# Layer norm without its division: mean only in the norm, the weight folded into the next weights, the division on the last pass's sums, and GpSimd alone for block preparation and residual adds

## The chip, the cores and the metric

One core of one Trainium2 chip. The metric is the device time of one launch in microseconds, the median of several runs. TensorE is called PE here, VectorE DVE, ScalarE ACT, GpSimd POOL or GpSimd, and SP is the engine whose queue issues the DMAs.

## The reference, cut to what matters

```
x = attention(q, k, v), keys and values pooled by 8      (8 batches, 576 tokens, 512 columns)
u = x + (x^T U V)^T                                       (mixing along the tokens, rank 32)
x = u + max(u w1, 0) w2                                   (layer 0: 512 -> 2048 -> 512)
mu = mean(x); var = mean((x - mu)^2)                      (along the 512 columns)
xn = (x - mu) / sqrt(var + 1e-6) * g
out = x + max(xn w1', 0) w2'                              (layer 1: 512 -> 2048 -> 512)
```

All in float32. The scale of a token is positive, so max(s a, 0) = s max(a, 0): the division by the root can stand before or behind layer 1.

## The kernel before, in words

The 4608 tokens stand on the free axis, the 512 columns as 4 chunks (NCC) of 128 partitions. A float32 product is made of three matmuls on rounded parts, high times high, low times high and high times low; `split` makes the high part by a rounding copy (on ACT or DVE) and the low part by a subtraction (on DVE or GpSimd).

Phase A (up to about 650 us) computes attention, the token mixing and the first 8 of the 16 hidden blocks of layer 0. `ahead` decodes later weights from float64 words and stores them in DRAM (`w_d`).

Then come three passes, each over 9 groups of 512 tokens (TG): pass 0 is the other half of layer 0, passes 1 and 2 are the halves of layer 1. A group has 4 units, a unit being two hidden blocks. `unit` makes the first product of a unit by a scheme with 7 block products instead of 8 (42 matmuls of 256 columns into the PSUM tiles `pa` and `pbc`, with the joins on DVE at lines 1315 and 1321, the activations on ACT at 1279 and their low parts on DVE at 1285). `second` issues the 24 matmuls of the second product (512 columns, PSUM tiles `py`) one unit later, between those of the next `unit`. So a unit is 66 matmuls. The join of line 1321 reads and writes the PSUM tile into which the last block product then adds: PE waits there for DVE.

- `group_prep` loads a group (`xraw`), makes the differences of blocks (line 1212, tiles `t3`, `t2` and `xraw`) and the 7 pairs of parts `op`. There are 16 `op` buffers and a group takes 14, so most of the next group's parts are made while the last unit of the present one runs.
- `residual` loads `res` and `yt` and adds them (line 1397). `finish` adds the four PSUM sums (line 1360) and stores. Pass 0 stores to `x_d`, pass 1 keeps its partial sum in `p_d`, pass 2 adds everything and writes the output.
- `norm` treats a group of pass 0 during the next group, in two halves of 256 tokens: sum of the chunks, split, mean by two matmuls with a matrix of 1/512 (lines 1418 and 1419), subtraction (1442), squares on ACT and their sum (1453, 1454), the same two matmuls again, then a root on ACT (1461), a reciprocal on DVE (1466), one correcting step (1468 to 1474) and a multiplication by the weight g and the reciprocal (1481). The result goes to `n_d`, from which passes 1 and 2 read.

The order of all instructions is made by the class `Order` while the program is built: each operation has a cost for every engine that may take it, a due time that follows the PE work recorded so far, and the buffers that it holds; the planner simulates queues and buffers and issues whatever is ready with the earliest due time, on the engine that would end it first. The engines then run these lists in order; what waits at the head of a list holds up all behind it.

Of the kernel before, what the change touches and what calls it, by code (L numbers as in the profile page):

```python
# [386 lines left out]

class Kern:
    def __init__(self, nc, tc, aps):
# [62 lines left out]
        for a in ("lnh", "lnl"):  # L452
            ring(b2, a, [128, TH], F32R)
        for a in ("lns", "lnq", "lnm", "lnv", "lnd"):
            ring(b2, a, [128, TH])
# [8 lines left out]
    def setup(self, ctx):  # L464
# [9 lines left out]
        self.eps = cp.tile([128, 1], F32, tag="eps", name="eps")  # L474
        nc.gpsimd.memset(self.eps, 1e-6)
        self.neg_b = cp.tile([128, 1], F32, tag="negb", name="neg_b")
# [9 lines left out]
        self.p_d = [dp.tile([128, NCC, TG], F32, tag=f"p_d{g}", name=f"p_d{g}") for g in range(NG)]  # L486
        self.w_d = {}
# [195 lines left out]
    def ahead(self, layer, f, z):  # L683

        x = self.decoded(layer, f, z)
        self.wd[layer, f, z] = d = Buf(None)
# [516 lines left out]
    def group_prep(self, p, g):  # L1203
# [24 lines left out]
        def sp(k):  # L1228
# [6 lines left out]
            self.split(View(hl[0], None, view), View(hl[1], None, view), src, TG)  # L1235
# [129 lines left out]
    def residual(self, p, g):  # L1365
# [27 lines left out]
        )  # L1393
        for c in range(NCC):
            o.op(
                {GP: c_pool(TG), DVE: c_dve(TG)},
# [5 lines left out]
    def norm(self, g):  # L1402

        nc, o = self.nc, self.o
        x = self.res[g]
        steps = []
        eng = {GP: c_pool(TH), DVE: c_dve(TH)}
        for z in range(2):
            t = slice(z * TH, z * TH + TH)
            b = {}  # L1410

            def total(b=b):
                hi, lo, ps = self.buf("lnh"), self.buf("lnl"), self.buf("pbc")
                whole = lambda t: t
                self.split(View(hi, None, whole), View(lo, None, whole), View(b["s"], None, whole), TH)

                def mm(e):
                    e.matmul(ps.t[:, :TH], self.ones, hi.t, start=True, stop=False)
                    e.matmul(ps.t[:, :TH], self.ones, lo.t, start=False, stop=True)

                o.op({PE: c_pe(TH, 2)}, mm, r=[hi, lo], w=[ps])
                return ps

            def n0(b=b, t=t):
                s, q = b["s"], b["q"] = self.buf("lns"), self.buf("lnq")
                o.op(eng, lambda e: e.tensor_add(s.t, x.t[:, 0, t], x.t[:, 1, t]), r=[(x, 0), (x, 1)], w=[s])
                o.op(eng, lambda e: e.tensor_add(q.t, x.t[:, 2, t], x.t[:, 3, t]), r=[(x, 2), (x, 3)], w=[q])
                o.op(eng, lambda e: e.tensor_add(s.t, s.t, q.t), r=[q], w=[s])

            def n2(b=b, t=t, total=total):  # L1430
                ps = total()
                mu = self.buf("lnm")
                o.op(
                    {ACT: c_act(TH, True), DVE: c_dve(TH)},
                    lambda e: copy(nc, e, mu.t, ps.t[:, :TH]),
                    r=[ps],
                    w=[mu],
                )
                for c in range(NCC):
                    o.op(  # L1440
                        eng,
                        lambda e, c=c: e.tensor_sub(x.t[:, c, t], x.t[:, c, t], mu.t),
                        r=[mu],
                        w=[(x, c)],
                    )

            def n4(b=b, t=t):
                s = b["s"] = self.buf("lns")
                sq = {ACT: c_act(TH)}
                o.op(sq, lambda e: e.activation(s.t, x.t[:, 0, t], AF.Square), r=[(x, 0)], w=[s])  # L1450
                for c in range(1, NCC):
                    q = self.buf("lnq")
                    o.op(sq, lambda e, c=c, q=q: e.activation(q.t, x.t[:, c, t], AF.Square), r=[(x, c)], w=[q])
                    o.op(eng, lambda e, q=q: e.tensor_add(s.t, s.t, q.t), r=[q], w=[s])

            def n6(b=b, total=total):
                ps = total()
                sd, ve = b["sd"], b["ve"] = self.buf("lnd"), self.buf("lnv")
                o.op(
                    {ACT: c_act(TH, True) + 40},  # L1460
                    lambda e: e.activation(sd.t, ps.t[:, :TH], AF.Sqrt, bias=self.eps),
                    r=[ps],
# [144 lines left out]
```

## Time and profile before

| | |
|---|---|
| median of 3 runs | 1839.62 us (1839.45 to 1840.44) |
| profiled execution, its own time | 1839.23 us |
| its span, first to last instruction | 1837.4 us |
| PE busy / weight loads | 1769.2 us (96%) / 1619.5 us (88%) |
| DVE busy | 1279.1 us (70%), 2512 instructions |
| ACT busy | 723.4 us (39%), 2047 instructions |
| GpSimd busy | 435.6 us (24%), 446 instructions |
| pass 0, 1 and 2 begin (first matmul of line 1257 in each) | 652.4, 1063.8 and 1448.6 us |

Busy is the time in which an engine executes; a PE that is busy at the lower of its two clocks counts as busy. Share of busy time alone does not say where the time goes: the stages differ, and the table of windows and the list of waits tell them apart.

### The profile page before, as it was taken

The numbers are of one execution on the slowest core, as the hardware profiler recorded it, in microseconds if no ns is written. First come the engines' busy times: TensorE is split into PE (matmuls) and PEld (weight loads), VectorE is DVE, ScalarE is ACT, GpSimd is POOL, SyncE is SP. The second block draws the span as 40 slices with busy tenths as digits, with TensorE's granted clock in tenths as the row PEclk, the third lists the DMA queues.
The fourth block names the chain that finished last, engine by engine and source line by source line (L and its number), as shares of the span: only waits on it lengthen the run. The fifth ranks groups of instructions, "written<-read, shape, count | busy, mean of one in ns | idle before, by whom it ended". The sixth has DMA issues, their size and how long they took to land.

```text
span 1837.4 us, 30175 instructions
## 1 busy us (share of the span) xinstructions
PE 1769.2 (96%) x11482; PEld 1619.5 (88%) x11482; DVE 1279.1 (70%) x2512; ACT 723.4 (39%) x2047; POOL 435.6 (24%) x446
## 2 busy tenths in 40 slices
PE   5689999999999999999999999999999999999999
PEld 4579999999999998888888888999999999999998
DVE  7987888888855577888888898776434754454443
ACT  4445655655644233333333453333332432222221
POOL 2242322323310122222222331111111321111110
PEclk7689999999999999999999999999999999999999
DMA  6434444444411352333333334434111433222211
GB/s 179 152 114 154 137 153 155 138 154 149 124 62 46 111 192 81 115 115 115 115 115 115 115 127 138 132 127 142 53 64 58 160 116 115 93 92 92 98 64 47
DMA packets 88642, 212.42 MB, mean 116 GB/s; under 512 B 9264, under 2 KB 17456, under 8 KB 82736
## 3 DMA queue, kind: packets, MB, share of 16 engines
q1 hardware_dynamic: 88352, 210.49, 34.8%
q8 instruction: 90, 1.47, 0.3%
q14 instruction: 56, 0.46, 0.1%
q10 hardware_dynamic: 144, 0.00, 0.0%
HBM read 141.25 MB, written 69.21 MB: 115 GB/s over the span
## 4 chain that ended last, share of the span: by engine, by line
PE 87%; DVE 9%; DMA 1%; ACT 1%; issue 1%; POOL 0%; SPq 0%; DVEq 0%; ACTq 0%; POOLq 0%
PE py L1345 30%; PE pa L1257 15%; PE pbc L1257 12%; PE pa L1027 11%; PE pbc L1060 10%; PE py L378 3%; PE py L767 2%; PE py L871 1%; DVE lnv L1468 1%; DVE res L1481 1%; DVE lnd L1466 1%; PE py L889 1%; PE py L890 1%; PE py L928 0%; DMA v<-v 0%
## 5 line engine op out<-in xcount | busy, mean ns | idle before, releaser
L1345 PE MATMUL py<-hid,w2h 128*128 128x512 f32 x1728 | 546.4, 398 | 0.0
L1257 PE MATMUL pa<-op,w1h 128*128 128x256 f32 x1728 | 328.5, 282 | 21.5 <-DVE pa L1321 19.8
L1257 PEld LDWEIGHTS pa<-op,w1h 128*128 128x128 f32 x1728 | 294.0, 189 | 59.4 <-DVE pa L1321 22.6
L1345 PE MATMUL py<-hid,w2l 128*128 128x512 f32 x864 | 337.9, 391 | 0.0
L1345 PEld LDWEIGHTS py<-hid,w2h 128*128 128x128 f32 x1728 | 278.7, 191 | 13.4
L1257 PE MATMUL pbc<-op,w1h 128*128 128x256 f32 x1296 | 247.2, 283 | 1.3 <-ACT s L383 0.6
L1257 PEld LDWEIGHTS pbc<-op,w1h 128*128 128x128 f32 x1296 | 221.9, 190 | 28.5 <-DVE lnv L1465 0.8
L1257 PE MATMUL pa<-op,w1l 128*128 128x256 f32 x864 | 244.2, 283 | 0.0
L1027 PE MATMUL pa<-hid,wh 128*128 128x288 f32 x1024 | 220.1, 307 | 8.9 <-DVE op L1039 8.8
L1060 PE MATMUL pbc<-op,wh 128*128 128x288 f32 x1024 | 215.8, 303 | 0.0
L1315 DVE TENSOR_TENSOR pbc<-s,pbc 128x512 f32<-128x512 f32 x108 | 74.8, 692 | 183.2 <-PE pbc L1257 183.1
L1345 PEld LDWEIGHTS py<-hid,w2l 128*128 128x128 f32 x864 | 163.4, 189 | 36.6
L1257 PE MATMUL pbc<-op,w1l 128*128 128x256 f32 x648 | 183.7, 283 | 0.0
L1027 PEld LDWEIGHTS pa<-hid,wh 128*128 128x128 f32 x1024 | 167.1, 192 | 12.3 <-DVE op L1039 8.7
L1279 ACT ACTIVATE hid<-pbc 128x512 fp32r<-128x512 f32 x108 | 64.7, 599 | 266.4 <-DVE pbc L1315 265.6
L1060 PEld LDWEIGHTS pbc<-op,wh 128*128 128x128 f32 x1024 | 163.7, 188 | 4.4 <-issue 2.8
L1257 PEld LDWEIGHTS pa<-op,w1l 128*128 128x128 f32 x864 | 163.4, 189 | 0.0
L1027 PE MATMUL pa<-hid,wl 128*128 128x288 f32 x512 | 153.3, 299 | 0.4 <-POOL wl L508 0.4
L1060 PE MATMUL pbc<-op,wl 128*128 128x288 f32 x512 | 150.9, 295 | 0.0
L383 ACT COPY s<-pa 128x256 f32<-128x256 f32 x200 | 74.3, 372 | 146.3 <-PE pa L1257 144.1
L508 POOL TENSOR_TENSOR op<-t,op 128x512 fp32r<-128x512 f32 x26 | 35.2, 1356 | 393.0 <-DVE op L385 312.5
L1279 ACT ACTIVATE hid<-pa 128x512 fp32r<-128x512 f32 x108 | 64.5, 597 | 156.3 <-PE pa L1257 149.4
(189 smaller groups left out, 3135.3 us busy)
## 6 DMA issues: line engine op xcount, KB each, us to landing
xraw<-n_d SPq DMA_DIRECT2D x18, 1024.0 KB, 4.8
wraw<-wC SPq DMA_DIRECT2D x32, 512.0 KB, 4.1
wraw<-wA SPq DMA_DIRECT2D x24, 512.0 KB, 4.3
w_d<-wx SPq DMA_DIRECT2D x48, 256.0 KB, 4.0
wraw<-w_d SPq DMA_DIRECT2D x48, 256.0 KB, 3.7
k<-kT SPq DMA_DIRECT2D x32, 288.0 KB, 3.7
q<-qT SPq DMA_DIRECT2D x32, 288.0 KB, 3.2
v<-v SPq DMA_DIRECT2D x32, 288.0 KB
```

The costliest lines, as they stand in the source:

```text
L378: e.matmul(out, src, ident, start=first, stop=True, is_transpose=True, skip_group_check=True)
L383: e.copy(dst, src)
L508: lambda e: e.tensor_sub(lo(), src(), hi().bitcast(F32)),
L767: lambda e: e.matmul(ps.t[:, i : i + 2 * SP], q.t[:, QT[t] : QT[t] + 128], kbd.t.rearrange("p h n -> p (h n)"), start=True, stop=True, ski ...
L871: lambda e: e.matmul(ps.t[:, :SH], vs.t[:, w], ef.t[:, h, c], start=(h == 0), stop=(h == 1)),
L889: e.matmul(ps.t[:, :SH], w, eh.t[:, h, c], start=True, stop=False)
L1027: e.matmul(ps.t[:, :SH], w.t[:, c], u, start=(i == 0), stop=(i == 3 * NCC - 1))
L1060: e.matmul(ps.t[:, :SH], w.t[:, c], x, start=(f == 0 and j == 0), stop=(f == NA - 1 and j == 2))
L1257: e.matmul(bank.t[:, sl], w.t[:, self.WCOL[k], c], u.t[:, t], start=(first and i == 0), stop=(last and i == 5), skip_group_check=True,)
L1279: lambda e: e.activation(h.t[:, :TG], bank.t, AF.Relu),
L1315: o.op({DVE: c_dve(TG)}, lambda e: e.tensor_add(c.t, s.t, c.t), r=[s], w=[c])
L1345: e.matmul(y.t, w.t[:, i, c], x.t[:, :TG], start=(first and q == 0), stop=(last and q == 2))
```

## The change

- The norm takes off only the mean and works on whole groups. Its sums, the low part and the sums of squares are GpSimd's alone, the high part and the squares ACT's, the four subtractions DVE's, straight from PSUM; `n_d` is written before the squares.
- The variance comes from four float32 matmuls per group, each with 128 tokens as weights and one column of 1/512, so that it stands on the partitions as 128 x 4. Root, reciprocal and correction work on 128 x 4. The result goes to DRAM (`r_d`).
- `ahead` multiplies the first weights of layer 1 by g.
- In pass 2 `residual` no longer adds; it loads `r_d`, spread over all partitions (tile `lns`). `finish` adds the PSUM sum to pass 1's sum (DVE), multiplies by the reciprocal and adds the residual (GpSimd; in the last group GpSimd or DVE).
- Block differences and low parts of `group_prep` are GpSimd's alone, high parts ACT's alone (except for the first group); the residual add of pass 0 is GpSimd's alone.

```diff
 def ahead(self, layer, f, z):
+        if layer == 1 and z == 0:
+            for c in range(NCC):
+                self.o.op(
+                    {ACT: c_act(128), DVE: c_fast(128)},
+                    lambda e, c=c: scale(self.nc, e, x.t[:, c * 128 : c * 128 + 128], self.g_sb[:, c : c + 1]),
...
 def group_prep(self, p, g):
+        first = p == 0 and g == 0
+        on = {GP: c_pool(TG), DVE: c_dve(TG)} if first else {GP: c_pool(TG)}
...
-            o.op({GP: c_pool(TG), DVE: c_dve(TG)}, lambda e: e.tensor_sub(dst(), a(), c()), r=r, w=w)
+            o.op(on, lambda e: e.tensor_sub(dst(), a(), c()), r=r, w=w)
...
+            hi, lo = ((ACT, DVE), (DVE, GP)) if first else ((ACT,), (GP,))
+            self.split(View(hl[0], None, view), View(hl[1], None, view), src, TG, hi_on=hi, lo_on=lo)
...
 def finish(self, p, g, dc, y):
         else:
-            o.op({DVE: c_dve(TG)}, lambda e: e.tensor_add(r.t[:, dc], r.t[:, dc], y.t), r=[y], w=[(r, dc)])
-            dst, d = (self.x_d, self.xd) if p == 0 else (self.out, {})
+            t, q = self.part[g]
+            on = {GP: c_pool(TG)} if g < NG - 1 else {GP: c_pool(TG), DVE: c_dve(TG)}
+            o.op({DVE: c_dve(TG)}, lambda e: e.tensor_add(t.t[:, dc], t.t[:, dc], y.t), r=[y], w=[(t, dc)])
+            o.op(on, lambda e: e.tensor_mul(t.t[:, dc], t.t[:, dc], q.t), r=[q], w=[(t, dc)])
+            o.op(on, lambda e: e.tensor_add(r.t[:, dc], r.t[:, dc], t.t[:, dc]), r=[(t, dc)], w=[(r, dc)])
+            dst, d = self.out, {}
...
 def residual(self, p, g):
+        if p == 2:
+            q = self.buf("lns")
+            o.op({SY: 450}, lambda e: e.dma_start(q.t, self.r_d[g].to_broadcast([128, TG])),
...
-                {GP: c_pool(TG), DVE: c_dve(TG)},
+                {GP: c_pool(TG)},
                 lambda e, c=c: e.tensor_add(r.t[:, c], r.t[:, c], y.t[:, c]),
...
 def norm(self, g):
+        eng = {GP: c_pool(TG)}
+        def n0():
+            o.op(eng, lambda e: e.tensor_add(s.t, x.t[:, 0], x.t[:, 1]), r=[(x, 0), (x, 1)], w=[s])
+            o.op(eng, lambda e: e.tensor_add(q.t, x.t[:, 2], x.t[:, 3]), r=[(x, 2), (x, 3)], w=[q])
+            o.op(eng, lambda e: e.tensor_add(s.t, s.t, q.t), r=[q], w=[s])
+        def n1():
+            self.split(View(hi, None, whole), View(lo, None, whole), View(s, None, whole), TG, hi_on=(ACT,), lo_on=(GP,))
+            def mm(e):
+                e.matmul(ps.t, self.ones, hi.t, start=True, stop=False)
+                e.matmul(ps.t, self.ones, lo.t, start=False, stop=True)
+            for c in range(NCC):
+                o.op({DVE: c_dve(TG)}, lambda e, c=c: e.tensor_sub(x.t[:, c], x.t[:, c], ps.t), r=[ps], w=[(x, c)])
+            o.op({SY: 450}, lambda e: e.dma_start(self.n_d[g], x.t), r=[x], w=[d], size=4 * 262144)
+        def n2():
+            o.op(sq, lambda e: e.activation(s.t, x.t[:, 0], AF.Square), r=[(x, 0)], w=[s])
+            for c in range(1, NCC):
+                o.op(sq, lambda e, c=c, q=q: e.activation(q.t, x.t[:, c], AF.Square), r=[(x, c)], w=[q])
+                o.op(eng, lambda e, q=q: e.tensor_add(s.t, s.t, q.t), r=[q], w=[s])
+        def n3():
+                for i in range(nt):
+                    e.matmul(ps.t[:, i : i + 1], s.t[:, i * 128 : i * 128 + 128], self.mean, start=True, stop=True,
...
+            o.op({ACT: 150}, lambda e: e.activation(sd.t, part(), AF.Sqrt, bias=self.eps), r=[ps], w=[sd])
+            o.op({DVE: 130}, lambda e: e.tensor_scalar_add(ve.t, part(), 1e-6), r=[ps], w=[ve])
+            o.op({DVE: 95}, lambda e: e.reciprocal(sd.t, sd.t), w=[sd])
+            for _ in range(2):
+                o.op(small, lambda e: e.tensor_mul(ve.t, ve.t, sd.t), r=[sd], w=[ve])
+            o.op(small, lambda e: e.tensor_scalar(ve.t, ve.t, -0.5, 1.5, op0=ALU.mult, op1=ALU.add), w=[ve])
+            o.op(small, lambda e: e.tensor_mul(sd.t, sd.t, ve.t), r=[ve], w=[sd])
```

How the planner's lists move is shown at three places. In the changed kernel lines 1338, 1344, 1308 and 1383 are what 1315, 1321, 1285 and 1360 were; 520 is the low part (508 before) and 1234 the block difference (1212 before).

First, DVE in pass 0 where a norm ends and the next joins of a unit follow. Before (1465 reads the variance from PSUM, 1466 is the reciprocal, 1481 the scaling):

```order
L1465 TENSOR_SCALAR lnv_6936<-pbc_234 128x256
L1466 RECIPROCAL lnd_6937<-lnd_6937 128x256
L1468 TENSOR_TENSOR lnv_6936<-lnv_6936,lnd_6937 128x256 x2
L1471 TENSOR_SCALAR lnv_6936<-lnv_6936 128x256
L1474 TENSOR_TENSOR lnd_6937<-lnd_6937,lnv_6936 128x256
L1481 SCALAR_TENSOR_TENSOR res_6928<-res_6928,g_sb,lnd_6937 128x256 x4
L1315 TENSOR_TENSOR pbc_233<-s_6924,pbc_233 128x512
L1360 TENSOR_TENSOR res_6929<-res_6929,py_237 128x512
L1321 TENSOR_TENSOR pa_231<-s_6926,pa_231 128x256
```

And with the change, at the same place of a group:

```order
L1500 TENSOR_SCALAR lnv_6977<-pbc_244 128x4
L1501 RECIPROCAL lnd_6978<-lnd_6978 128x4
L1503 TENSOR_TENSOR lnv_6977<-lnv_6977,lnd_6978 128x4 x2
L1504 TENSOR_SCALAR lnv_6977<-lnv_6977 128x4
L1505 TENSOR_TENSOR lnd_6978<-lnd_6978,lnv_6977 128x4
L1338 TENSOR_TENSOR pbc_243<-s_6966,pbc_243 128x512
L1383 TENSOR_TENSOR res_6970<-res_6970,py_247 128x512
L1344 TENSOR_TENSOR pa_241<-s_6968,pa_241 128x256
```

The block stands ahead of the joins as it did, once per group and not twice, with 4 elements per partition instead of 256, and without the four scalings.

Second, GpSimd from one block difference of a group to the norm's sums of squares. Before (1426 and 1427 are sums of the norm, half a group each):

```order
L1212 TENSOR_TENSOR t_6337<-xraw_6336 128x512
L508 TENSOR_TENSOR op_192<-xraw_6336,op_191 128x512
L1212 TENSOR_TENSOR xraw_6336<-xraw_6336 128x2x256
L1426 TENSOR_TENSOR lns_6933<-res_6928 128x256
L1427 TENSOR_TENSOR lnq_6934<-res_6928 128x256
L1442 TENSOR_TENSOR res_6928<-res_6928,lnm_6935 128x256 x2
L1454 TENSOR_TENSOR lns_6933<-lns_6933,lnq_6934 128x256
```

With the change (1458 to 1460 are the norm's sums, 1484 the sums of squares):

```order
L1234 TENSOR_TENSOR t_6375<-xraw_6374 128x512
L520 TENSOR_TENSOR op_202<-xraw_6374,op_201 128x512
L1234 TENSOR_TENSOR xraw_6374<-xraw_6374 128x2x256
L1458 TENSOR_TENSOR lns_6975<-res_6970 128x512
L1234 TENSOR_TENSOR t_6376<-xraw_6374 128x512
L1459 TENSOR_TENSOR lnq_6976<-res_6970 128x512
L1234 TENSOR_TENSOR xraw_6374<-xraw_6374,t_6376 128x2x256
L1460 TENSOR_TENSOR lns_6975<-lns_6975,lnq_6976 128x512
L520 TENSOR_TENSOR lnl_6974<-lns_6975,lnh_6973 128x512
L1484 TENSOR_TENSOR lns_6975<-lns_6975,lnq_6976 128x512 x3
```

The norm's sums and the block differences now alternate in one list. PE has the two matmuls of the mean (lines 1468 and 1469), which need `lnl`, behind the second unit of the group, and the four of the variance (line 1491) behind the fourth.

Third, DVE's last instructions of the program. Before:

```order
L1285 SCALAR_TENSOR_TENSOR hid_206<-pa_232,hid_205 128x512
L1360 TENSOR_TENSOR res_6929<-res_6929,py_237 128x512
L1360 TENSOR_TENSOR res_6929<-res_6929,py_238 128x512
L1360 TENSOR_TENSOR res_6929<-res_6929,py_236 128x512
L1360 TENSOR_TENSOR res_6929<-res_6929,py_235 128x512
```

With the change:

```order
L1388 TENSOR_TENSOR yt_6972<-yt_6972,py_247 128x512
L1388 TENSOR_TENSOR yt_6972<-yt_6972,py_248 128x512
L1388 TENSOR_TENSOR yt_6972<-yt_6972,py_246 128x512
L1388 TENSOR_TENSOR yt_6972<-yt_6972,py_245 128x512
L1390 TENSOR_TENSOR res_6970<-res_6970,yt_6972 128x512 x2
L1389 TENSOR_TENSOR yt_6972<-yt_6972,lns_6975 128x512 x2
L1390 TENSOR_TENSOR res_6970<-res_6970,yt_6972 128x512 x2
```

Behind the four PSUM sums there are six more operations on DVE; the first two multiplications are GpSimd's.

## Rows read from the trace of the kernel before

**Rows 1.** The page's first line.

```profile
span 1837.4 us, 30175 instructions
```

**Rows 2.** Windows: length, then busy time (instructions) per engine, granted clock, DMA share, GB/s.

```profile
652.00:1060.00 408.00, 388.17 (x2396) 348.72 (x2395) 333.40 (x583) 154.72 (x348) 122.12 (x122) 0.98 0.35 118
1060.00:1110.00 50.00, 47.53 (x296) 42.44 (x295) 47.23 (x96) 22.94 (x51) 17.10 (x13) 1.00 0.39 127
...
1160.00:1760.00 600.00, 600.00 (x3758) 540.95 (x3757) 316.29 (x550) 178.24 (x367) 113.72 (x92) 1.00 0.30 103
```

**Rows 3.** Waits of PE, 640 to 1110 us: total, times, longest.

```profile
PE pa L1257 <- DVE pa L1321: 19.8, 10, 2.4
```

**Rows 4.** Timeline of DVE, 737 to 751 us: start, length in us, instruction, idle before.

```profile
740.47 1.75 DVE L1466 RECIPROCAL lnd<-lnd 128x256 f32<-128x256 f32 x1 [0.54 <-ACT lnd L1461]
742.26 2.86 DVE L1468 TENSOR_TENSOR lnv<-lnv,lnd 128x256 f32<-128x256 f32 x2
745.15 1.27 DVE L1471 TENSOR_SCALAR lnv<-lnv 128x256 f32<-128x256 f32 x1
...
746.92 1.67 DVE L1481 SCALAR_TENSOR_TENSOR res<-res,g_sb,lnd 128x256 f32<-128x256 f32 x4
748.51 0.69 DVE L1315 TENSOR_TENSOR pbc<-s,pbc 128x512 f32<-128x512 f32 x1
...
749.71 0.42 DVE L1321 TENSOR_TENSOR pa<-s,pa 128x256 f32<-128x256 f32 x1
```

**Rows 5.** Timeline of PE, 749 to 751 us.

```profile
750.18 0.51 PE L1257 MATMUL pa<-op,w1h 128*128 128x256 f32 x2 [2.31 <-DVE pa L1321]
```

**Rows 6.** Windows, the five us behind that wait.

```profile
749.50:754.50 5.00, 4.32 (x18) 3.93 (x19) 5.00 (x10) 1.55 (x5) 1.47 (x2) 0.66 1.04 375
```

**Rows 7.** Timeline of GpSimd, 741 to 748 us.

```profile
742.12 1.29 POOL L1212 TENSOR_TENSOR t<-xraw 128x512 f32<-128x512 f32 x1 [5.53 <-DMA xraw<-u_d]
...
744.80 1.47 POOL L1212 TENSOR_TENSOR xraw<-xraw 128x512 f32<-128x512 f32 x1
```

**Rows 8.** Instructions of the tile lnd: count, then ns least/median/most.

```profile
L1468 DVE TENSOR_TENSOR lnv<-lnv,lnd x28: 409/1202/1509, 720.4 to 1127.2; 128x256 f32<-128x256 f32 x28
```

**Rows 9.** Timeline of DVE in pass 2, around the end of a group.

```profile
1539.56 0.70 DVE L1315 TENSOR_TENSOR pbc<-s,pbc 128x512 f32<-128x512 f32 x1 [1.42 <-PE pbc L1257]
...
1540.90 0.43 DVE L1321 TENSOR_TENSOR pa<-s,pa 128x256 f32<-128x256 f32 x1
...
1541.84 1.28 DVE L1360 TENSOR_TENSOR res<-res,py 128x512 f32<-128x512 f32 x2
1543.69 0.69 DVE L1360 TENSOR_TENSOR res<-res,py 128x512 f32<-128x512 f32 x1 [0.58 <-PE py L1345]
```

**Rows 10.** Timeline of GpSimd there: first and last of four instructions without a pause.

```profile
1538.22 1.28 POOL L1212 TENSOR_TENSOR xraw<-xraw 128x512 f32<-128x512 f32 x1 [5.67 <-DVE t L1212]
...
1542.08 1.29 POOL L1212 TENSOR_TENSOR xraw<-xraw,t 128x512 f32<-128x512 f32 x1
```

**Rows 11.** Timeline of ACT in pass 2: the high part of a block.

```profile
1572.73 0.61 ACT L383 CAST op<-xraw 128x512 fp32r<-128x512 f32 x1
```

**Rows 12.** Timeline of PE: the norm's two matmuls, then matmuls of 512 columns.

```profile
739.07 0.28 PE L1418 MATMUL pbc<-lnh,ones 128*128 128x256 f32 x1
...
739.30 0.63 PE L1345 MATMUL py<-hid,w2h 128*128 128x512 f32 x2
739.77 0.40 PE L1345 MATMUL py<-hid,w2l 128*128 128x512 f32 x1
```

**Rows 13.** Timeline of PE in phase A: four plain float32 matmuls of 128 columns.

```profile
204.50 0.60 PE L378 MATMUL py<-ident,sc 128*72 128x128 f32 x4
```

**Rows 14.** Line 767, plain float32 too: count, ns least/median/most, first and last start.

```profile
L767 PE MATMUL py<-kbd,q x320: 283/286/609, 5.0 to 559.6; 128*128 128x144 f32 x160
```

**Rows 15.** Timeline of DVE: the last adds of the program.

```profile
1831.68 2.73 DVE L1360 TENSOR_TENSOR res<-res,py 128x512 f32<-128x512 f32 x4 [2.73 <-PE py L1345]
```

**Rows 16.** Timeline of DVE: three adds of SBUF tiles, GpSimd idle.

```profile
669.93 1.89 DVE L1397 TENSOR_TENSOR res<-res,yt 128x512 f32<-128x512 f32 x3
```

More of the change, by code (lines that the diff above doesn't have):

```diff
@@ L486, in setup @@
         self.p_d = [dp.tile([128, NCC, TG], F32, tag=f"p_d{g}", name=f"p_d{g}") for g in range(NG)]
+        self.r_d = [dp.tile([1, TG], F32, tag=f"r_d{g}", name=f"r_d{g}") for g in range(NG)]
         self.w_d = {}
@@ L1393, in residual @@
         )
+        if p == 2:
+            q = self.buf("lns")
+            o.op(
+                {SY: 450},
+                lambda e: e.dma_start(q.t, self.r_d[g].to_broadcast([128, TG])),
+                r=[self.rd[g]],
+                w=[q],
+                size=262144,
+            )
+            self.part[g] = y, q
+            return
         for c in range(NCC):
             o.op(
-                {GP: c_pool(TG), DVE: c_dve(TG)},
+                {GP: c_pool(TG)},
                 lambda e, c=c: e.tensor_add(r.t[:, c], r.t[:, c], y.t[:, c]),
@@ L1405, in norm @@
         x = self.res[g]
[L1406 to L1444, printed above, removed]
-                    )
[L1447 to L1462, printed above, removed]
-                    w=[sd],
-                )
-                o.op({DVE: c_dve(TH)}, lambda e: e.tensor_scalar_add(ve.t, ps.t[:, :TH], 1e-6), r=[ps], w=[ve])
-                o.op({DVE: 1670}, lambda e: e.reciprocal(sd.t, sd.t), w=[sd])
-                for _ in range(2):
-                    o.op(eng, lambda e: e.tensor_mul(ve.t, ve.t, sd.t), r=[sd], w=[ve])
-                o.op(
-                    {DVE: c_fast(TH)},
-                    lambda e: e.tensor_scalar(ve.t, ve.t, -0.5, 1.5, op0=ALU.mult, op1=ALU.add),
-                    w=[ve],
-                )
-                o.op(eng, lambda e: e.tensor_mul(sd.t, sd.t, ve.t), r=[ve], w=[sd])
-            def n9(b=b, t=t, z=z):
-                sd = b["sd"]
-                for c in range(NCC):
-                    o.op(
-                        {DVE: c_dve(TH) + 60},
-                        lambda e, c=c: e.scalar_tensor_tensor(
-                            x.t[:, c, t], x.t[:, c, t], self.g_sb[:, c : c + 1], sd.t, op0=ALU.mult, op1=ALU.mult
-                        ),
-                        r=[sd],
-                        w=[(x, c)],
-                    )
-                if z == 1:
-                    self.nd[g] = d = Buf(None)
-                    o.op({SY: 450}, lambda e: e.dma_start(self.n_d[g], x.t), r=[x], w=[d], size=4 * 262144)
-            steps += [n0, n2, n4, n6, n9]
@@ new lines, in n2, with mm @@
+        def n2():
+            s = b["s"] = self.buf("lns")
+            sq = {ACT: c_act(TG)}
+            o.op(sq, lambda e: e.activation(s.t, x.t[:, 0], AF.Square), r=[(x, 0)], w=[s])
+            for c in range(1, NCC):
+                q = self.buf("lnq")
+                o.op(sq, lambda e, c=c, q=q: e.activation(q.t, x.t[:, c], AF.Square), r=[(x, c)], w=[q])
+                o.op(eng, lambda e, q=q: e.tensor_add(s.t, s.t, q.t), r=[q], w=[s])
+        def n3():
+            s, ps, sd, ve = b["s"], self.buf("pbc"), self.buf("lnd"), self.buf("lnv")
+            def mm(e):
+                for i in range(nt):
+                    e.matmul(
+                        ps.t[:, i : i + 1], s.t[:, i * 128 : i * 128 + 128], self.mean, start=True, stop=True,
+                        skip_group_check=True,
+                    )
+            o.op({PE: nt * 240}, mm, r=[s], w=[ps])
+            part = lambda: ps.t[:, :nt]
+            small = {DVE: 70}
+            o.op({ACT: 150}, lambda e: e.activation(sd.t, part(), AF.Sqrt, bias=self.eps), r=[ps], w=[sd])
[5 more added lines that the diff above has]
+            o.op(small, lambda e: e.tensor_mul(sd.t, sd.t, ve.t), r=[ve], w=[sd])
+            self.rd[g] = d = Buf(None)
+            o.op(
+                {SY: 450},
+                lambda e: e.dma_start(self.r_d[g].rearrange("o (i p) -> p (o i)", p=128), sd.t),
+                r=[sd],
+                w=[d],
+                size=32768,
+            )
@@ L1494, in passes @@
+        return [n0, n1, n2, n3]
     def passes(self):
```

32 lines of the change are left out of this document (26 added, 6 removed).

## The prediction

> **What bounds the kernel now.** I read the table of windows first. From 1160 to 1760 us (passes 1 and 2) PE is busy all the time: 3758 matmuls in 600 us, 0.1597 us each, so 66 x 0.1597 = 10.54 us for a unit and 42.2 us for a group [rows 2]. No change beside PE can win anything there. From 652 to 1110 us, which is pass 0 and the first units of pass 1, it is different: PE is busy 388.2 + 47.5 of 458 us, so it stands for 22.3 us, and the granted clock is 0.98 of full speed in pass 0, which is worth 0.02 x 408 = 8.2 us [rows 2]. DVE is busy 82% there (333 of 408 us) and 53% in the later window. The matmul count says the same: 2692 matmuls in 458 us, of which 70 are the norm's at about 0.12 us (8 us) and 2622 at 0.1597 (419 us, less 1.7 for the first unit, which has no second product beside it) make 425 us: 33 us are lost. I take **31 us** as what pass 0 and the start of pass 1 lose, with 27 and 33 as ends.
>
> The list of waits says to whom: 19.8 us are waits for the join of line 1321 on DVE, 10 of them, up to 2.4 us long [rows 3]. The timeline of DVE shows one from the inside. The reciprocal takes 1.75 us, the two multiplications behind it 2.86, the next operation 1.27, four scalings 1.67; only then come the joins of lines 1315 and 1321, both ready long before [rows 4]. PE resumes at 750.18 after 2.31 us of idleness [rows 5], and in the five us around that the granted clock is 0.66 of full, so for most of them PE ran at the lower of its levels [rows 6]. The multiplications are slow because GpSimd is at work: its instructions of 1.29 to 1.47 us fill 742.1 to 746.3 [rows 7], and each DVE operation between tiles in SBUF ends only when a GpSimd instruction has; the same multiplication takes 0.41 us at best and 1.20 in the median [rows 8]. DVE operations that read PSUM are not held up: joins take 0.70 and 0.43 us [rows 9] beside a busy GpSimd [rows 10]. So this stage is bounded by the norm's work in DVE's list and by its collisions with GpSimd.
>
> **The change, part by part.** *The norm on DVE.* The reciprocals of 256 elements, the scalings and most of the split and sum operations leave DVE; so do its share of block differences, parts and residual adds. Per group there remain four subtractions from PSUM (about 4 x 0.63 = 2.5 us at the pace of [rows 16]) and six operations on 4 elements. The subtractions come when the third unit of a group begins, and the next joins are due 6.6 and 7.9 us into a unit (1539.56 and 1540.90 against a unit that begins at 1533.0, since the add at 1543.69 waits for the last matmul of the unit before and so stands 0.2 us into the next [rows 9]): they fit. Of the small operations four work between SBUF tiles and can each wait for one GpSimd instruction: 4 x 1.29 = 5.2 us [rows 10]. They start about 1.3 us into the unit (last block product, activation, root), end by 6.5, and the join is due at 6.6. So this just fits, and GpSimd is not busy throughout. Hence the 31 us go. The Trainium skill (SBUF — State Buffer, "SBUF: two separate sides") says that a DVE operation with two SBUF inputs and a GpSimd operation take one port pair by an exclusive lock, for the whole instruction; the trace agrees (0.41 against 1.20 us). By that rule the small operations cost what GpSimd's cost, without it under 1 us; the sum is the same, the margin is not.
>
> *What remains of the stalls.* The weights of passes 0 and 1 are still split and combined on DVE and GpSimd in the first two groups of pass 0 and around the start of pass 1, now beside a busier GpSimd. Nothing in the rows gives this; between 0 and 15 us (half of what is lost today), I take **5 us**, nearer to the lower end, because nearly all of today's waits stand at one line and DVE loses most of what stood ahead of it.
>
> *GpSimd.* In a group of pass 0 it now has 4 block differences, 7 low parts, 4 residual adds, 3 sums, 1 low part and 3 sums of squares: 22 instructions of 512 elements at 1.29 us [rows 10], 28 us of 42.2, or 67% against 30% today (122 of 408 us [rows 2]). What PE waits for is its chain to the mean: the last finishing add ends 0.9 us into the second unit (1543.69 + 0.69 [rows 9]), and the two matmuls of the mean stand at that unit's end, 9.7 us later. If GpSimd begins the sums only then, six instructions and one rounding copy on ACT follow, 6 x 1.29 + 0.61 = 8.4 us [rows 10, 11]: 1.3 us to spare. If it begins with the first two sums, as their inputs allow, there are 3.9. The low parts of the next group are needed from 1.4 us after a group begins, and their buffers come free from 0.7 us into the last unit: seven low parts and a difference, 10.3 us, in a unit of 10.5, each due a unit later. I cost GpSimd at nothing; its cover is this margin. The variance's four matmuls stand two units behind the mean, for a chain of about 2.5 + 8 us, so they wait for nobody. The Trainium skill (GPSIMD Engine Reference, "Engine selection") advises against elementwise work on GpSimd, which it puts at about half of VectorE's speed; the trace agrees (1.29 against 0.63 us). By the rule alone, the moved work would cost twice as much; in the sum it costs nothing, since it leaves the engine that PE waits for.
>
> *PE.* Eight norm matmuls per group at 0.115 us (739.07 to 739.30 for two) make 0.92; now two of 512 columns at 0.235 (739.30 to 739.77 for two) make 0.47 [rows 12], and four plain float32 ones. Four of these start within 0.33 us of each other [rows 13], 0.11 each, and line 767's 160 matmuls in the program are 320 in the trace [rows 14]: 8 x 0.11 = 0.88. That is +0.43 per group, **+3.9 us** for nine. Ends: 4 x 0.11, so nothing gained or lost (0), and 8 x 0.19, the length of a weight load, +9.
>
> *The end.* Today the last four adds end at 1834.41 [rows 15] and the output's last DMA 3 us later. Now they are followed on DVE by six operations at 0.63 us [rows 16], 3.8 us, and the first must let GpSimd's second multiplication end (two from about 1832.4: 1835.0): **+4.4 us**, 3.8 to 5.
>
> *Costed at nothing.* 64 multiplications of weights by g, on ACT or DVE, in the background; 9 stores and 9 loads of `r_d` with tens of us of slack; ACT's high parts (0.61 us [rows 11]); pass 2's multiplications and adds on GpSimd (8 per group, 19 in all, 24.5 us of 42.2), since the PSUM tiles are released by DVE's add as before.
>
> **The sum**, against the profiled execution: 1837.4 [rows 1] - 31 + 5 + 3.9 + 4.4 = 1819.7 us of span. Its own time is 1.8 us above the span and the median 0.4 above that: **1822 us**.
>
> **The rivals.** *GpSimd late, slower than before.* If GpSimd's list, two thirds full, runs more than 1.3 to 3.9 us behind, PE stands at the mean's matmuls in each of the nine groups, and all behind it. For: in order, with DMA loads and ACT's copies ahead of its instructions; collisions stretch an instruction to 1.47 us [rows 7]. Against: DVE's SBUF work, with which it collides, is mostly gone. 5 us late past the margin, 9 x (5 + 1.7 for the lower clock) = 60 us, give 1882; it decides from 1 us past it, where 9 us would be lost (1831), and from 2.2 us past it the gain is gone (9 x 2.2 = 20).
>
> *The small operations hold the joins.* If four GpSimd instructions in a row hold them, and the first is late by one more, the join of line 1344 comes about 1 us late in each group: 9 us, 1831 us; with the lower clock behind each (1.7 us), 1846 us. For: three multiplications took 4.1 us in [rows 4]. Against: GpSimd waits for loads at that place today (5.53 us [rows 7]).
>
> *The weights keep pass 1's start as it is, and the first groups.* Then 12 to 15 us of the 31 stay: 1830 us.
>
> *The stalls only move* (no change within 0.2%, some 3.7 us, which is what a measurement of this kernel can tell from none): another wait takes all of the gain.
>
> **How the numbers follow.** Forecast 0.68; weights or small operations at 1831 0.18; GpSimd late enough to be slower 0.08; moved stalls 0.06. The forecast's own range is 1811 (all 33 us gone, matmuls and end at their lower ends: 1837.4 - 33 + 0 + 0 + 3.8 + 2.2 = 1810.4) to 1828; with the third case it reaches to 1834. Faster 0.86, same 0.05, slower 0.09.
>
> **What would show it.** Right: in the windows of pass 0 PE busy all but a few us and the clock at 1.00; no waits for the join's line; about 42.9 us per group; four small DVE operations with lengths near 1.3 us; the last DVE operation 4 to 5 us behind the last PSUM add. Wrong: waits of PE at line 1469 for GpSimd (the slower rival), at 1280 for 1344 with the small operations ahead of it on DVE, or at 1280 for line 520 on GpSimd; a clock still below 1.00 in pass 0; or stalls in pass 2, where the rows show none to lose.

## The result and the profile after

The changed kernel takes **1811.62 us** (median of 4 runs, 1811.12 to 1814.44), beside 1839.53 us (4 runs, 1835.34 to 1840.44) for the kernel before, measured again with it: ratio 0.9856, 95% interval 0.9838 to 0.9874. 1822 was predicted, with 1811 to 1828 as the forecast's own range and up to 1834 with the third rival; the sign was right, and the time is 0.6 us above the low end. A second measurement of the same kernel gave 1812.14 us, ratio 0.9866 (0.9852 to 0.9880).

The page of the changed kernel, first line and part 1:

```profile
span 1809.3 us, 30011 instructions
PE 1753.5 (97%) x11500; PEld 1609.4 (89%) x11500; DVE 1049.5 (58%) x2078; ACT 738.3 (41%) x2013; POOL 786.9 (43%) x682
```

DVE is 230 us less busy, GpSimd 351 us more, and the span is 28.1 us shorter [rows 1]. So the time does not follow the sum of the work. The table of windows of the changed kernel (columns as in [rows 2]) says where it came from:

```profile
652.00:1060.00 408.00, 406.95 (x2571) 367.13 (x2570) 211.41 (x346) 150.13 (x295) 271.67 (x211) 1.00 0.47 130
1060.00:1110.00 50.00, 49.64 (x313) 44.47 (x313) 32.94 (x63) 21.26 (x43) 21.34 (x16) 1.00 0.53 154
1160.00:1760.00 600.00, 599.74 (x3765) 540.57 (x3764) 235.87 (x410) 198.78 (x386) 286.30 (x222) 1.00 0.28 98
```

In the first two windows PE now stands for 1.4 us where it stood for 22.3, and the clock of the first is 1.00 where it was 0.98. In the third it was busy all the time before and is so now but for 0.3 us, with 7 matmuls more in 600 us. All waits of PE from 640 to 1130 us in the changed kernel (total, times, longest), against the 19.8 us of [rows 3]:

```profile
PE pa L1280 <- DVE pa L1344: 1.0, 1, 1.0
PE pa L1280 <- DVE s L385: 0.4, 1, 0.4
```

The first matmul of each pass and of each group stands in the trace. From one to the next, in us:

| | before | after |
|---|---|---|
| first matmul of pass 0, 1, 2; end of span | 652.4, 1063.8, 1448.6; 1837.4 | 650.4, 1035.9, 1417.1; 1809.3 |
| groups of pass 0 | 40.05, 44.48, 47.22, 47.26, 45.53, 47.25, 47.21, 47.11, 45.28 | 38.26, 43.29, then 43.42 seven times |
| first two groups of pass 1, then each | 46.07, 43.62, then 42.16 | 44.07, 42.14, then 42.07 (one of 42.59) |

The eleven groups that hold the norm, or the start of pass 1, took 501.1 us and take 471.7: **29.4 us less**, though their norm matmuls are longer. The end got 4.2 us longer, the start is 2.1 us earlier. That makes 27.3 of the 28.1; 0.8 is spread over the 15 groups between. The first group of pass 1 is the least steady: in the second profile of the same kernel it takes 45.75 us, not 44.07.

The norm's small operations in the changed kernel, timeline of DVE (columns as in [rows 4]); the unit begins at 731.9:

```profile
732.82 0.16 DVE L1500 TENSOR_SCALAR lnv<-pbc 128x4 f32<-128x4 f32 x1 [0.88 <-ACT lnd L1499]
732.90 0.17 DVE L1501 RECIPROCAL lnd<-lnd 128x4 f32<-128x4 f32 x1
733.10 2.15 DVE L1503 TENSOR_TENSOR lnv<-lnv,lnd 128x4 f32<-128x4 f32 x2
735.29 0.17 DVE L1504 TENSOR_SCALAR lnv<-lnv 128x4 f32<-128x4 f32 x1
735.49 0.16 DVE L1505 TENSOR_TENSOR lnd<-lnd,lnv 128x4 f32<-128x4 f32 x1
738.61 0.70 DVE L1338 TENSOR_TENSOR pbc<-s,pbc 128x512 f32<-128x512 f32 x1 [2.96 <-PE pbc L1280]
...
739.95 0.43 DVE L1344 TENSOR_TENSOR pa<-s,pa 128x256 f32<-128x256 f32 x1
```

In [rows 4] the joins started 11.6 and 12.8 us into the unit, after the norm (that unit begins at 737.0); now they start at 6.7 and 8.0, and DVE waits 2.96 us for PE instead. Two of the small operations are held up: 2.15 us for two multiplications of 4 elements per partition (2.56 in the six groups behind this one).

GpSimd's chain to the mean in the same group, timeline of GpSimd; its unit begins at 742.5:

```profile
741.64 1.29 POOL L1458 TENSOR_TENSOR lns<-res 128x512 f32<-128x512 f32 x1 [0.85 <-DVE res L1383]
742.89 1.30 POOL L1234 TENSOR_TENSOR t<-xraw 128x512 f32<-128x512 f32 x1
744.15 1.29 POOL L1459 TENSOR_TENSOR lnq<-res 128x512 f32<-128x512 f32 x1
745.39 1.29 POOL L1234 TENSOR_TENSOR xraw<-xraw,t 128x512 f32<-128x512 f32 x1
746.65 1.30 POOL L1460 TENSOR_TENSOR lns<-lns,lnq 128x512 f32<-128x512 f32 x1
748.68 1.29 POOL L520 TENSOR_TENSOR lnl<-lns,lnh 128x512 fp32r<-128x512 f32 x1 [0.73 <-ACT lnh L383]
```

and PE's matmul with that low part, timeline of PE:

```profile
753.31 0.39 PE L1469 MATMUL pbc<-lnl,ones 128*128 128x512 f32 x1
```

The low part ends at 749.97 and is wanted at 753.31: **3.3 us of margin**, the same in six of the nine groups and 2.5 to 3.9 in the others. GpSimd does start with the first sum before the last finishing add, as the prediction's upper case had it.

The end, timelines of DVE and then GpSimd, after the last matmul's end at 1801.31:

```profile
1802.02 1.76 DVE L1390 TENSOR_TENSOR res<-res,yt 128x512 f32<-128x512 f32 x2
1803.70 1.28 DVE L1389 TENSOR_TENSOR yt<-yt,lns 128x512 f32<-128x512 f32 x2
1804.91 1.28 DVE L1390 TENSOR_TENSOR res<-res,yt 128x512 f32<-128x512 f32 x2
```

```profile
1800.11 2.52 POOL L1389 TENSOR_TENSOR yt<-yt,lns 128x512 f32<-128x512 f32 x2 [28.18 <-DVE yt L1388]
```

DVE ends 4.9 us behind the last matmul; before it was 0.7 us ([rows 15]: 1834.41, its last matmul 1833.69).

### The profile page after: what moved, and what is told of

Its sections match the earlier page's. It is cut to its first block, busy times and chain, and to the rows that moved or that the text cites. A ratio compares the mean times of both kernels' runs of the same rounds, so it can differ in the third digit from the quotient of the medians.

```text
span 1809.3 us, 30011 instructions
## 1 busy us (share of the span) xinstructions
PE 1753.5 (97%) x11500; PEld 1609.4 (89%) x11500; DVE 1049.5 (58%) x2078; ACT 738.3 (41%) x2013; POOL 786.9 (43%) x682
## 4 chain that ended last, share of the span: by engine, by line
PE 92%; DVE 5%; DMA 2%; POOL 1%; issue 0%; SPq 0%; ACT 0%; DVEq 0%; POOLq 0%
PE py L1368 32%; PE pa L1280 17%; PE pbc L1280 12%; PE pbc L1079 11%; PE pa L1046 11%; PE py L378 3%; PE py L786 2%; PE py L908 1%; PE py L909 1%; DMA v<-v 1%; PE py L946 1%; PE py L947 0%; PE py L890 0%; PE py L975 0%; PE pbc L1491 0%
## 5 line engine op out<-in xcount | busy, mean ns | idle before, releaser
L520 POOL TENSOR_TENSOR op<-xraw,op 128x512 fp32r<-128x512 f32 x130 | 173.9, 1340 | 275.0 <-ACT op L383 270.8
L1368 PEld LDWEIGHTS py<-hid,w2h 128*128 128x128 f32 x1728 | 274.0, 189 | 11.0 <-DVE hid L1308 0.3
L1046 PEld LDWEIGHTS pa<-hid,wh 128*128 128x128 f32 x1024 | 166.8, 192 | 12.8 <-DVE op L1058 8.7
L1308 DVE SCALAR_TENSOR_TENSOR hid<-pa,hid 128x512 fp32r<-128x512 f32 x108 | 74.5, 690 | 125.6 <-ACT hid L1302 125.5
```

What stands on the lines that cost most here:

```text
L520: lambda e: e.tensor_sub(lo(), src(), hi().bitcast(F32)),
L1046: e.matmul(ps.t[:, :SH], w.t[:, c], u, start=(i == 0), stop=(i == 3 * NCC - 1))
L1308: lambda e: e.scalar_tensor_tensor(l.t[:, :TG], bank.t, 0.0, h.t[:, :TG].bitcast(F32), op0=ALU.max, op1=ALU.subtract),
L1368: e.matmul(y.t, w.t[:, i, c], x.t[:, :TG], start=(first and q == 0), stop=(last and q == 2))
```

## The experiments

The theory: pass 0 was bounded by the norm's work in DVE's list, and that work's collisions with GpSimd. The rivals: that the assignment to GpSimd alone (block preparation, residual adds) brings the gain; and that GpSimd's load is what now nearly costs it. A third one no run tests by itself: each edit makes the planner draw up a new order, and the order may bring part of a gain. Only in experiment 4 do DVE, ACT and PE execute the same lists as in the changed kernel.

**1. Each half of the change alone.** First the new norm with the assignments undone (an edit of the changed kernel):

```diff
-        on = {GP: c_pool(TG), DVE: c_dve(TG)} if first else {GP: c_pool(TG)}
+        on = {GP: c_pool(TG), DVE: c_dve(TG)}
-            hi, lo = ((ACT, DVE), (DVE, GP)) if first else ((ACT,), (GP,))
+            hi, lo = (ACT, DVE), (DVE, GP)
-                {GP: c_pool(TG)},
+                {GP: c_pool(TG), DVE: c_dve(TG)},
```

> The changed kernel with one half undone: block differences, low and high parts of block preparation and the residual adds of pass 0 may go to DVE or GpSimd (ACT or DVE) again, as before; the new norm stays. Theory A (what held PE was the norm's block of long and colliding operations ahead of the joins in DVE's list): almost all of the gain stays, 1810 to 1817 us, waits of PE for the join's line under 5 us in pass 0. Theory B (DVE was relieved by giving preparation and residual adds away): little of it stays, 1828 us or more, with 12 us or more of those waits.

1823.31 us, ratio 0.9938 (0.9923 to 0.9952): less than half of the gain, and in the range of neither theory. Its steady groups take 44.07 us, the first two of pass 1 47.27 and 43.91. Waits of PE, 640 to 1130 us:

```profile
PE pa L1280 <- DVE pa L1344: 7.3, 11, 2.0
PE py L1368 <- DVE hid L1308: 3.0, 2, 2.2
```

Then the assignments alone, with the old norm (an edit of the kernel before, the same three places the other way).

> The kernel before with the other half alone: block preparation and residual adds by GpSimd and ACT only (but for the first group), the old norm. Theory A: the reciprocals, their colliding followers and the scalings still stand ahead of the joins, and GpSimd, busier, collides more: 1833 to 1843 us, 12 us or more of PE waits for the join's line. Theory B: 1820 us or less, waits under 5 us.

1835.51 us, ratio 1.0005 (0.9996 to 1.0015): no change. Waits of PE there:

```profile
PE pa L1261 <- DVE pa L1325: 6.7, 7, 1.6
PE pbc L1423 <- DVE lnl L508: 5.0, 8, 1.4
PE py L1349 <- DVE hid L1289: 3.7, 1, 3.7
PE pbc L1422 <- DVE lnh L385: 2.7, 4, 1.8
PE pbc L1261 <- POOL op L508: 1.0, 1, 1.0
PE pa L1261 <- POOL op L508: 0.9, 1, 0.9
```

The join's waits fall from 19.8 to 6.7 us, and 13.3 us come back at the norm's own matmuls (lines 1422 and 1423), at a low part of `hid` and at GpSimd's block parts: here the stalls do only move. So the second half is worth nothing by itself and 12 to 15 us beside the first (1823.31 - 1811.62 makes 11.7, the eleven groups 13.3, the two ratios 15); the halves don't add. The Trainium skill (Perfetto Trace Analysis, "Optimizing Scalar/DVE Operations") says that handing work from DVE to GpSimd might not help, as they share a port; this run agrees, with no change from it; beside the new norm the same step is worth those 12 to 15 us, so there it does help.

**2. Which of the two assignments.** The changed kernel with only the residual add of pass 0 open to DVE again (the third place of the edit above), and with only the block preparation open (the first two).

> The changed kernel with only the residual adds of pass 0 open to DVE again. Undoing both assignments cost 11.7 us (1823.3 against 1811.6). If the residual adds are most of it: 1819 us or more. If the preparation of blocks is: 1811 to 1814 us, groups of pass 0 at 43.4 us.

> The changed kernel with only the block preparation (differences, high and low parts) open to DVE again, residual adds GpSimd's alone. If preparation is most of the 11.7 us: 1818 to 1824 us, waits of PE for the join behind long rows of low parts on DVE. If the residual adds are: below 1815 us.

1809.86 us, ratio 0.9847 (0.9819 to 0.9876), and 1817.30 us, ratio 0.9888 (0.9852 to 0.9924). So the residual add's assignment is worth nothing; the preparation's is worth 6 to 7 us by the medians (against 1811.62 and against the other run of the pair), though with two runs each the intervals overlap. In both runs the steady groups stay at 43.42. With the preparation open the loss stands at the first group (41.44 against 38.26) and at the second of pass 1 (43.48 against 42.14), 4.5 us in all; the first group of pass 1 takes 45.67, which is within what this group scatters. At these places DVE also prepares weights. One lies in the first group of this run, timeline of DVE and then of PE:

```profile
681.07 1.78 DVE L520 TENSOR_TENSOR op<-t,op 128x512 fp32r<-128x512 f32 x1
682.77 2.38 DVE L520 TENSOR_TENSOR w2l<-wraw,w2h 128x512 fp32r<-128x512 f32 x2
685.07 0.68 DVE L520 TENSOR_TENSOR op<-xraw,op 128x512 fp32r<-128x512 f32 x1
685.67 0.68 DVE L1338 TENSOR_TENSOR pbc<-s,pbc 128x512 f32<-128x512 f32 x1
686.27 0.42 DVE L1344 TENSOR_TENSOR pa<-s,pa 128x256 f32<-128x256 f32 x1
```

```profile
686.74 0.80 PE L1280 MATMUL pa<-op,w1h 128*128 128x256 f32 x2 [2.26 <-DVE pa L1344]
```

Block parts and weight parts stand ahead of the joins. The 0.65 us more per steady group in the run with the new norm and both assignments open (experiment 1) do not appear here; neither assignment alone makes them.

**3. Which part of the old norm.** Edits of the kernel before. First the reciprocal and the whole correcting step are left out, with its preparation:

```diff
-                o.op({DVE: c_dve(TH)}, lambda e: e.tensor_scalar_add(ve.t, ps.t[:, :TH], 1e-6), r=[ps], w=[ve])
-                o.op({DVE: 1670}, lambda e: e.reciprocal(sd.t, sd.t), w=[sd])
-                for _ in range(2):
-                    o.op(eng, lambda e: e.tensor_mul(ve.t, ve.t, sd.t), r=[sd], w=[ve])
...
-                o.op(eng, lambda e: e.tensor_mul(sd.t, sd.t, ve.t), r=[ve], w=[sd])
```

> The kernel before without the reciprocal and its correcting step (seven operations per half group; the root itself is then used as the factor); everything else, the scalings and the engines' choice too, as before. Theory A, in the form that the block's length ahead of the joins is what counts: the waits fall from 19.8 us to under 6 us, the clock in pass 0 is 1.00, 1812 to 1822 us. If instead DVE's total load or the scalings decide, over half of the waits stay and the time is above 1826 us.

1813.42 us, ratio 0.9882 (0.9867 to 0.9897). Then only the reciprocal's line is left out, and then only the correcting step with its preparation, while the reciprocal stays:

> The kernel before without the reciprocal alone; the correcting step (four operations between SBUF tiles, two of them open to GpSimd) stays and works on the root. If the reciprocal's own 1.75 us, twice per group, is what PE waits for: the waits for the join's line fall below 8 us and the time to 1813 to 1821 us. If the collisions of the operations behind it weigh as much: 8 to 15 us of waits stay and 1822 to 1832 us.

> The kernel before without the correcting step and the operation that prepares it; the reciprocal stays. If the reciprocal's length decides: over 12 us of waits stay, 1828 us or more. If the colliding operations decide (2.86 + 1.27 us in the stall shown): waits below 8 us, 1813 to 1822 us.

1810.79 us, ratio 0.9854 (0.9836 to 0.9872), and 1807.39 us, ratio 0.9836 (0.9818 to 0.9854). **Either alone brings at least as much as both**, and more than either expectation had. The waits for the join's line that are left in the three runs, in this order (PE, 640 to 1130 us; 19.8 in [rows 3]):

```profile
PE pa L1257 <- DVE pa L1321: 4.6, 5, 2.0
PE pa L1257 <- DVE pa L1321: 3.6, 3, 1.9
PE pa L1257 <- DVE pa L1321: 3.4, 3, 1.9
```

The steady groups of the last two take 43.11 us, which is the 42.16 of a group without stalls and the norm's 0.92 of matmuls. So the time does not fall in proportion to what is left out: once the block ends ahead of the joins, leaving out more wins nothing. The run without the correcting step has the lowest median of all; it has neither the longer end (4.2 us) nor the longer norm matmuls (3.1 us) of the change. The norm's block without the reciprocal, timeline of DVE (the unit begins at 865.1), then GpSimd's:

```profile
867.19 0.89 DVE L1467 TENSOR_TENSOR lnv<-lnv,lnd 128x256 f32<-128x256 f32 x2 [0.54 <-ACT lnd L1461]
868.11 0.29 DVE L1470 TENSOR_SCALAR lnv<-lnv 128x256 f32<-128x256 f32 x1
868.44 0.43 DVE L1473 TENSOR_TENSOR lnd<-lnd,lnv 128x256 f32<-128x256 f32 x1
868.90 1.67 DVE L1480 SCALAR_TENSOR_TENSOR res<-res,g_sb,lnd 128x256 f32<-128x256 f32 x4
...
871.92 0.70 DVE L1315 TENSOR_TENSOR pbc<-s,pbc 128x512 f32<-128x512 f32 x1 [0.74 <-PE pbc L1257]
```

```profile
871.25 1.29 POOL L1212 TENSOR_TENSOR xraw<-xraw 128x512 f32<-128x512 f32 x1 [6.24 <-DVE t L1212]
```

The two multiplications take 0.89 us here and 2.86 in [rows 4], the next operation 0.29 against 1.27. GpSimd is idle beside them: here it starts 6.2 us into the unit, when the block is done, and in [rows 7] at 5.2 us, when the block (reciprocal at 3.5 us) had its multiplications still ahead. But the reciprocal's absence is not all that differs, for the planner's order is new. In every steady group of these three runs the first block difference (`t`) is made by DVE, behind the block, and GpSimd starts only when it is there; before, GpSimd made it. And the block begins 1.4 us earlier (2.1 us into the unit against 3.5): the last sum of squares ahead of it ends 1.8 us before the unit begins, not 0.1. The same without the correcting step, reciprocal in place (unit from 862.2; DVE, then GpSimd):

```profile
863.89 1.75 DVE L1465 RECIPROCAL lnd<-lnd 128x256 f32<-128x256 f32 x1 [0.86 <-ACT lnd L1461]
...
869.04 0.70 DVE L1315 TENSOR_TENSOR pbc<-s,pbc 128x512 f32<-128x512 f32 x1 [0.64 <-PE pbc L1257]
```

```profile
868.48 1.29 POOL L1212 TENSOR_TENSOR xraw<-xraw 128x512 f32<-128x512 f32 x1 [6.34 <-DVE t L1212]
```

In both the join of line 1315 comes 6.8 us into the unit, when PE has its input ready, instead of 11.6. Is the removed work enough for that, without the new order? For the correcting step it is: from its first multiplication to the scalings the block of [rows 4] spends 4.66 us on it (742.26 to 746.92), more than the 2.31 us that PE waits [rows 5]. For the reciprocal it is not: 1.75 us less would leave 0.56 of that wait, so the rest is the new order and the collisions that it avoids. Leaving out both is not better than either because in every second steady group (44.05 us instead of 43.12) PE waits 0.7 us for the join of the second unit.

**4. GpSimd's margin.** The changed kernel, with the second of the norm's sums computed 3 and 5 times, which puts 2.5 and 5.0 us more on GpSimd ahead of the mean in every group (the lists of DVE, ACT and PE stay the same; the edit with 5 is shown):

```diff
-            o.op(eng, lambda e: e.tensor_add(q.t, x.t[:, 2], x.t[:, 3]), r=[(x, 2), (x, 3)], w=[q])
+            def second(e):
+                for _ in range(5):
+                    e.tensor_add(q.t, x.t[:, 2], x.t[:, 3])
+            o.op(eng, second, r=[(x, 2), (x, 3)], w=[q])
```

> The changed kernel with GpSimd's list made 2.5 us longer in each of the nine groups of the norm: its second sum is taken three times instead of once, the lists of all other engines stay word for word. The trace of the changed kernel shows the last low part done 3.3 us ahead of the mean's matmuls in the steady groups. Theory (GpSimd costs nothing as long as it is inside that margin): no change, within 3 us of the changed kernel. If GpSimd is already a bound: 9 x 2.5 = 23 us slower.

> The same with the second sum taken five times, 5.0 us longer per group. Theory: 5.0 - 3.3 = 1.7 us past the margin, so PE waits about 1.7 us at the mean's second matmul (line 1473 there) in each of some eight groups: 14 us slower, up to 25 with a lower clock behind each wait. If the margin can be made up elsewhere: no change; if GpSimd is already a bound: 9 x 5 = 45 us slower.

With 2.5 us: 1811.91 us, ratio 0.9861 (0.9832 to 0.9890), groups of 43.42, no change. With 5.0 us: 1839.57 us, ratio 1.0009 (0.9998 to 1.0021), **the whole gain gone**. The two largest waits of PE and the window of pass 0 of the second:

```profile
PE pbc L1473 <- POOL lnl L520: 8.6, 9, 1.3
PE pbc L1472 <- ACT lnh L383: 7.0, 8, 0.9
```

```profile
652.00:1060.00 408.00, 392.71 (x2394) 349.15 (x2394) 189.85 (x307) 138.65 (x272) 296.05 (x231) 0.97 0.45 121
```

5.0 less the margin of 3.3 makes 1.7 us in nine groups, 15.3; the waits at the mean's two matmuls are 15.6 (the first of them needs ACT's high part of GpSimd's sum, so it is late too). But the time rose by 27.7 (1839.57 - 1811.91, both measured beside the same runs of the kernel before), past the 25 expected at most: the granted clock of pass 0 is 0.97 instead of 1.00, which is worth 0.03 x 408 = 12.2 us. The prediction's formula for this rival, 9 x (time past the margin + 1.7 for the clock), gives 30.6.

**5. A shorter end.** The changed kernel; in the last group the kept sum is multiplied and added to the residual early, on GpSimd, so that behind the PSUM sum stand one multiplication and one add:

```diff
+            if g < NG - 1:
...
+            else:
+                o.op({DVE: c_dve(TG)}, lambda e: e.tensor_mul(t.t[:, dc], y.t, q.t), r=[y, q], w=[(t, dc)])
...
+            if g == NG - 1:
+                for c in range(NCC):
+                    o.op({GP: c_pool(TG)}, lambda e, c=c: e.tensor_mul(y.t[:, c], y.t[:, c], q.t), r=[q], w=[(y, c)])
+                    o.op({GP: c_pool(TG)}, lambda e, c=c: e.tensor_add(r.t[:, c], r.t[:, c], y.t[:, c]), r=[(y, c)], w=[(r, c)])
```

> The changed kernel with another end: in the last group the kept sum is multiplied and added to the residual early, on GpSimd, so that behind the last PSUM sums stand one multiplication from PSUM each and one add each, two of them on GpSimd. Theory: the six DVE operations behind the last PSUM read become two, 4 x 0.63 = 2.5 us less, 1808 to 1810 us. If the end is set by the output's DMAs instead, no change.

1809.60 us, ratio 0.9863 (0.9846 to 0.9879). Since 2 us are about what one measurement can tell, it was run again beside the changed kernel on one chip:

> The changed kernel once more, beside the next run on one chip: 1809 to 1815 us, the same groups of 43.4 us in pass 0. It is the measure for the kernel with the shorter end.

> The kernel with the shorter end once more: from its first look, whose last DVE operation stands 2 to 3 us behind the last matmul, 2 to 2.5 us below the changed kernel of the run beside it, more than the spread of either.

1812.14 us (1810.66 to 1816.74, ratio 0.9866) and **1808.51 us** (1807.25 to 1811.65, ratio 0.9847, 0.9833 to 0.9860). Its end, timeline of DVE:

```profile
1798.18 2.77 DVE L1392 TENSOR_TENSOR yt<-py,lns 128x512 f32<-128x512 f32 x4 [2.81 <-PE py L1368]
1800.86 1.76 DVE L1393 TENSOR_TENSOR res<-res,yt 128x512 f32<-128x512 f32 x2
```

Four multiplications from PSUM and two adds, the other two adds being GpSimd's: DVE ends 4.4 us after its first operation there, 6.9 in the changed kernel (1799.34 to 1806.19). The last group, from its first matmul to the end of the span, takes 53.5 us in both profiles of this version and 55.75 in both of the changed kernel, 2.3 us less. By this, and by the difference of the medians beside each other, 3.6, this version is faster than the changed kernel; the times alone don't settle it, since the two intervals of the ratio overlap and the first measurement's ratio (0.9863) is no lower than the changed kernel's (0.9856). What was not tried is this end together with the opened residual add of experiment 2, and the old norm without its correcting step together with the block preparation on GpSimd and ACT.

## Why the prediction was right, and where its sizes were off

- **What bounds pass 0**: right. Waits for the join fell from 19.8 us to 1.0 and the clock of that window rose to 1.00, as the last part of the prediction asked. Experiment 3 shows the cause: three ways to shorten the old norm's block, with nothing else of the change, bring 21 to 31 us against the kernel before measured beside them, where the whole change brings 26 to 28; the assignments with the whole old block bring nothing. What the block's length, its collisions with GpSimd and the planner's new order each bring is not shown; only for the correcting step is the removed work, 4.66 us, by itself more than the wait.
- **31 us lost**: too low. The eleven groups gained 29.4 us while their norm matmuls grew by 3.1, so 32.5 us of stalls went; with the 1.4 us that PE still waits, about 34 were there. The end of 33 was nearer than the value taken. The first group of pass 1 makes these numbers uncertain by 1 to 2 us.
- **5 us of stalls left**: the step that failed by most. 1.4 us were left. The prediction feared the weights' split at the first groups and at pass 1's start, "beside a busier GpSimd"; a loss there of about that size shows where the block preparation stays open to DVE (6 to 7 us by the medians of experiment 2, 4.5 in the two groups clear of scatter). It was the changed assignment of the preparation that cleared it.
- **Small operations**: two of four waited for GpSimd (0.90 and 1.22 us above, 1.34 and 1.22 in the next six groups), two did not (0.17 and 0.16), and all were to last near 1.3 us; they end 3.7 us into the unit, not at 6.5, and the rival in which they hold the joins did not come.
- **GpSimd's margin**, predicted as 1.3 to 3.9 us, is 3.3, and decides in the way that the slower rival said, but sooner: experiment 4 costs 27.7 us, the whole gain, at 1.7 us past it. The prediction had the gain gone from 2.2 us past it; there it left out the 1.7 us per group for the lower clock that it had counted a few words earlier.
- **PE's norm matmuls**: +3.9 us expected, +3.1 measured. The unit with the mean's two lasts 11.01 us against 10.54, 0.47 as taken; the one with the variance's four float32 matmuls 11.26, so 0.72 where 0.88 was taken. With 0.07 us on the group's first unit that makes 1.26 us per group against 0.92. The 42.9 us per group among the signs was mis-added: the prediction's own terms make 42.2 + 0.47 + 0.88 = 43.5, and 43.42 was measured.
- **The end**: +4.4 expected, +4.2 measured. **Passes 1 and 2**: nothing to gain, and their groups went from 42.16 to 42.07 us.
- **The start**: 2.1 us that the prediction has no term for. The first matmul of pass 0 stands between 648.0 and 653.0 us over all runs, at 650.4 and 649.3 in two runs of the changed kernel itself, and PE's list up to there is unchanged; it is scatter of a profiled execution.

In the span 1819.7 was predicted and 1809.3 measured. Of the 10.4 us, 6.5 are stalls (32.5 gone, 26 predicted), 2.1 the start, 0.8 the matmuls, 0.2 the end and 0.8 spread over the other groups. All of them point the same way, so the time came near the low end of the range; no two errors cancelled.

## What to carry to other kernels

When an engine off the critical path has a block of work with a due time, ask whether the block ends ahead of it, and look for the neighbour that starts while the block runs. Once the block is in time, shortening it further wins nothing, so two parts of a change need not add up: here leaving out the correcting step, or the reciprocal of 1.75 us with the new order that came with it, each removed all of the 4.1 us that a steady group lost (47.2 against 43.1). Before work is moved onto a slack engine, measure its margin at the place where the bounding engine waits, not its busy share: two thirds busy in pass 0 (271.67 of 408 us) with 3.3 us of margin cost nothing, and 5 us more per group cost all that the change had won.

## What had not been expected of the hardware

- A multiplication of 4 elements per partition waits for GpSimd like one of 256: 0.15 us at best, 1.22 in the median. Where the residual adds may go to DVE again (experiment 2) GpSimd is idle at that place and all 18 take 0.15 to 0.16 us, yet by the medians and their intervals no time clear of the noise is won by it. The row of line 1503 in the changed kernel, count and ns least/median/most:

```profile
L1503 DVE TENSOR_TENSOR lnv<-lnv,lnd x18: 149/1218/1339, 733.1 to 1082.5; 128x4 f32<-128x4 f32 x18
```

- An operation with a single input can be held too: the TENSOR_SCALAR of 256 elements took 0.29 us with GpSimd idle and 1.27 beside it [rows 4]. The Trainium skill (SBUF — State Buffer, "SBUF: two separate sides") lets a DVE operation in a 2-port performance mode take the shared lock too, and names a float32 copy, which has one input, as such a case; the trace agrees that one input is no protection, though no run here shows the mode. The reciprocal of 256 elements took 1.73 to 1.75 us in all 18 cases of the kernel before, also in the two in which GpSimd worked for 1.2 to 1.3 us of it (at 1102.1 and 1124.6 us), so it shows no such wait.
- In the run with 5.0 us more on GpSimd, seventeen waits of at most 1.3 us went with a granted clock of 0.97 instead of 1.00 over a 408 us window, and the time rose by 1.8 times the waits' own length (27.7 against 15.6 us).
